# Storing the third pair's rows and gathering the first expert's tokens one step earlier

## The chip, the cores and the metric

The kernel runs on one core of a Trainium2 chip. The metric is the time of one execution on the device in microseconds (us), as the median of several runs. Beside it stands one execution under the hardware profiler; its span runs from the first to the last instruction.

## The reference

Two blocks follow each other. The first is attention with a sliding window of 128 and a linear position bias: 8 batches, 8 heads, 576 positions, head dimension 64.

```python
scores = scale * np.matmul(q, k.transpose(0, 1, 3, 2))
scores = np.where(mask, scores + bias[None], -1e9)   # 0 <= rel < 128
attn = softmax(scores)
x = np.matmul(attn, v)                                # to (4608, 512)
```

The second is a mixture of 8 experts that drops no token. Each of the 4608 tokens goes to the one expert with the largest logit.

```python
logits = x @ w_gate
expert_idx = np.argmax(logits, axis=1)
h = np.maximum(x_sorted[lo:hi] @ w1[e], 0.0)          # 512 -> 1024
y_sorted[lo:hi] = h @ w2[e]                           # 1024 -> 512
out = gate_w[:, None] * y                             # gate_w: softmax probability of the chosen expert
```

## The kernel before

**Attention.** The work is cut into 16 units: 4 pairs of batches, and for each pair 4 pairs of heads. A unit has 4 groups of key blocks, so there are 64 steps, i = 4 x unit + group. In a step, PE forms the scores of the step two ahead (`scores`, L756), ACT takes their exponential (L762), DVE multiplies by the bias factors (L765, for the last group of a unit L770), and PE multiplies the probabilities of this step by the values (`values`, L791). Twice in a unit, at groups 2 and 3, `finish` copies the result to `xT` on ACT (L808, L810) and adds up the probabilities on PE (L823), which DVE takes into `sumT` (L834).

The order of all instructions is written out by hand: a manual schedule. Each engine runs its own instructions in that order, so one that waits holds back all later ones on its engine. PSUM tiles called `m` come from a pool of two (`ps_m`), and the score tiles `sp` from another pool of two.

**Work behind the attention.** When a pair is done, `behind(bp)` returns a list of portions, which `some()` takes one at a time, one in each of the next steps. They hold the routing of the pair that is done: gate logits (`gate`, L843, L848), their turning to token rows (`turn`, L867), the choice of the expert (`scale_a` to `scale_c`), the place of each token in its expert's list (`count`, `place`), one-hot matrices (`ones_at`, L974 to L983) and the lists themselves (`enlist`, matmuls at L993, sum at L1000).

They also hold the storing of the pair's 9 row tiles, of 128 tokens each. `row_turned` transposes four blocks on PE (L1007) and copies them to the tile `xs` on ACT (L1009). `row_out` adds the scales on POOL (L1016) and stores the tile to the DRAM tensor `x_rows` by a DMA that POOL issues (L1021, two for the last tile). `row(bp, t)` does both. The `xs` tiles come from a pool of 4, so tile t reuses the buffer of tile t - 4 and waits for its store.

For the third pair (`bp == 2`, whose portions run in steps i = 48 and on) the list is another one, because the first expert's tokens are taken from the first three pairs alone. `early_table` (a matmul at L1069, small DVE instructions L1071 to L1073, then L1040 to L1047) makes the list `g_idx`, and `gather` issues four indirect DMAs on POOL (L1152), each of which fetches 128 rows of `x_rows` into `xg`. The gather waits for all stores of rows and for `g_idx`.

**Tokens of the first expert.** In the last unit, `prepare(fixed[0])` adds portions: for each of the four gathered blocks a scaling on DVE (`to_scale`, L1164, tile `xn`) and a turning (`to_columns`: four transposes on PE at L1177, a copy to `xgT` on ACT at L1178), then four sums on DVE (L537 to L540). The scaling of block j + 1 shares a portion with the turning of block j. What is left of the portions after step 63 is run by `while tasks: some()`.

**Experts.** Each expert's two layers are Strassen products of 7 multiplications (`strassen1`, L1357 and L1414, into the PSUM tiles `pair0a` to `pair2b`; `strassen2`, L1469). During the first expert the routing of the fourth pair is done (`with_tail`). The load of the first expert's w2 (L565 on SP) follows the end of the attention, whose memory it takes over.

Of the kernel before, what the change touches and what calls it, by code (L numbers as in the profile page):

```python
# [457 lines left out]
def kernel(  # L458
# [25 lines left out]
    TPB = 2 * S // P  # L484
# [18 lines left out]
    x_d = nc.dram_tensor("x_rows", (N, NA * PW), F32, kind="Internal").ap()  # L503
    x_pieces = x_d.rearrange("n (a w) -> (n a) w", a=NA)

    with ExitStack() as fast:
# [50 lines left out]
        def load_w1(g, w_pool, parts=None):  # L557
            if "w1" not in g:
                g["w1"] = w_pool.tile([P, DB, F], F32, name="w1")
            a = parts or slice(0, DB)  # L560
            nc.sync.dma_start(g["w1"][:, a], g["src"][0].rearrange("(a p) f -> p a f", p=P)[:, a])
# [5 lines left out]
        fixed = [dict(e=e, n=NJ, c0=e * NJ, src=(moe_w1[e], moe_w2[e]), pool=mx_pool) for e in range(E)]  # L567
# [23 lines left out]
        units = [(bp, hp) for bp in range(BP) for hp in range(HP)]  # L591
# [22 lines left out]
        def load_part(u, g):  # L614
            if g == 0:
                load_k(u, 0, S, nc.sync)
            elif g == 1:
                load_q(u, 0, S, nc.sync)
            else:
                load_v(u, g - 2, nc.gpsimd if u in (6, 7) else nc.sync)  # L620
# [14 lines left out]
        def no_earlier_than(there):  # L635
            nc.sync.dma_start(pace[:], there)
# [53 lines left out]
        def placed(bp, t):  # L690

            b = 2 * bp * S
            if t < 8:
                return [(0, P, b + t // 4 * S + t % 4 * P)]
            return [(0, KB, b + 4 * P), (KB, KB, b + S + 4 * P)]
# [44 lines left out]
        def table_consts():  # L740
            K["cols"] = iota("cols", [P, P], [[1, P]], 0, 0)
            K["thr"] = iota("thr", [P, NF], [[P, NF]], CAP, 0)
            K["xth"] = iota("xth", [P, XU], [[1, XU]], 1, 0)
            K["e_of"] = iota("e_of", [P, E, NF], [[1, E], [0, NF]], 0, 0)
# [92 lines left out]
        def gate(bp, c):  # L837
            if bp not in gs:
                gs[bp] = xp.tile([P, 2 * S], F32, name="gs", bufs=1)
            ps = ps_m.tile([P, 512], F32, name="m")  # L840
            c0, n = ((0, LQ), (LQ, LQ), (2 * LQ, P))[c]
            for hp in range(HP):
                nc.tensor.matmul(  # L843
                    ps[32 * hp : 32 * hp + 32, :n], lhsT=wgd[:, hp, :], rhs=xT[bp][:, hp, c0 : c0 + n],
                    start=True, stop=True,
                )
            if c < 2:
                nc.vector.tensor_tensor(gs[bp][:, c0 : c0 + n], ps[:, :n], sumT[bp][:, :LQ], op=ALU.add)  # L848
            else:
                nc.vector.tensor_tensor(  # L850
                    gs[bp][:, c0 : c0 + n].rearrange("p (b q) -> p b q", b=2),
                    ps[:, :n].rearrange("p (b q) -> p b q", b=2),
                    sumT[bp][:, None, LQ:].to_broadcast([P, 2, S - LQ]), op=ALU.add,
                )
# [5 lines left out]
        def turn(bp, part):  # L860

            if part == 0:
                gsr[bp] = small.tile([P, TPB, P], F32, name="gsr")
            t0, n = ((0, 4), (4, 4), (8, 1))[part]
            ps = ps_m.tile([P, 512], F32, name="m")
            for k in range(n):
                nc.tensor.transpose(ps[:, k * P : (k + 1) * P], gs[bp][:, (t0 + k) * P : (t0 + k + 1) * P], ident[:])  # L867
            nc.scalar.copy(gsr[bp][:, t0 : t0 + n, :].rearrange("p t c -> p (t c)"), ps[:, : n * P])
# [135 lines left out]
        def row_turned(bp, t):  # L1004
            ps = ps_m.tile([P, 512], F32, name="m")
            for hp in range(HP):
                nc.tensor.transpose(ps[:, hp * P : (hp + 1) * P], xT[bp][:, hp, t * P : (t + 1) * P], ident[:])  # L1007
            xs = xs_of[bp, t] = rows.tile([P, NA, PW], F32, name="xs")
            nc.scalar.copy(  # L1009
                xs[:, :, :PD].rearrange("p a (h f) -> p h a f", h=HP), ps.rearrange("p (h a f) -> p h a f", h=HP, a=NA),  # L1010
            )

        def row_out(bp, t):

            xs = xs_of.pop((bp, t))
            nc.gpsimd.tensor_copy(  # L1016
                xs[:, :, PD:].rearrange("p (r x) h -> p r x h", r=2),
                es_of[bp][:, t].unsqueeze(2).to_broadcast([P, 2, 2, HP]),
            )
            for p0, n, r0 in placed(bp, t):  # L1020
                nc.gpsimd.dma_start(x_d[r0 : r0 + n, :], xs[p0 : p0 + n].rearrange("p a w -> p (a w)"))  # L1021

        def row(bp, t):
            row_turned(bp, t)
            row_out(bp, t)
# [113 lines left out]
        def in_rows(g):  # L1139
            return g["n"] == NJ and g["e"] < NR  # L1140

        def gather(g, src):
            nm = "" if g["n"] == NJ else "1"
            g["xg"] = g["pool"].tile([P, g["n"], NA, PW], F32, name="xg" + nm)
            for j in range(g["n"]):
                c = g["c0"] + j
                if in_rows(g):
                    todo = [(g["xg"][:, j].rearrange("p a w -> p (a w)"), src, g_idx[:, c : c + 1])]
                else:
                    todo = [(g["xg"][:, j, k, :], x_pieces, p_idx[:, c - NR * NJ, k : k + 1]) for k in range(NA)]  # L1150
                for to, where, idx in todo:
                    nc.gpsimd.indirect_dma_start(  # L1152
                        out=to, out_offset=None, in_=where, in_offset=bass.IndirectOffsetOnAxis(ap=idx, axis=0),
                    )
# [66 lines left out]
        def behind(bp):  # L1221

            g3 = [lambda k=k: gate(bp, k) for k in range(3)]
            t3 = [lambda k=k: turn(bp, k) for k in range(3)]
            rs = [lambda t=t: row(bp, t) for t in range(TPB)]
            a, b, c, n, p, o, e = (
                [lambda f=f: f(bp)] for f in (scale_a, scale_b, scale_c, count, place, ones_at, enlist)
            )
            if bp == 2:
                return [g3, t3, a, b + [lambda: row_turned(bp, 0)], c + n + [lambda: row_turned(bp, 1)],  # L1230
                        [lambda: row_turned(bp, 2)], p + [lambda t=t: row_out(bp, t) for t in range(3)], o + rs[3:4],
                        rs[4:6], e + rs[6:7], [early_table] + rs[7:9], [lambda: gather(fixed[0], x_d[: 3 * 2 * S, :])]]
            turned = [lambda t=t: row_turned(bp, t) for t in range(2)]
            outs = [lambda t=t: row_out(bp, t) for t in range(2)]
            return [g3[0:1], g3[1:2], g3[2:] + t3[0:1], t3[1:], a, turned[0:1], b, turned[1:2], c + n + outs,
                    rs[2:3], p + rs[3:4], rs[4:5], o, rs[5:6], rs[6:7], e + rs[7:9]]
# [3 lines left out]
        def some():  # L1240
            if tasks:
                for f in tasks.pop(0):
                    f()
# [10 lines left out]
        for i in range(NG):  # L1254
            u, g = divmod(i, 4)
            bp, hp = units[u]
            no_earlier_than(prob[min(i + 1, NG - 1)][0:1, 0, 0:1])
            if u + 2 < len(units):
                load_part(u + 2, g)
            if u in (5, 6) and g % 2 == 1:  # L1260
                d = 2 * (u - 5) + g // 2
                load_w1(fixed[0], w1_a, slice(d, d + 1))
            if i == 1:
                token_numbers()
                table_consts()
            if g == 2:
                values(u, 0, (4,))
                finish(u, 0)
                some()
            if i + AHEAD < NG:  # L1270
                scores(i + AHEAD)
            if u in (10, 11):
                ws_tasks.pop(0)()
            if g == 0:
                values(u, 0, (0, 1))
                if u < HP - 1:
                    factors(u + 1)
            elif g == 1:
                values(u, 0, (2, 3))
            elif g == 2:  # L1280
                values(u, 1, (3, 4, 5))
            else:
                values(u, 1, (6, 7, 8))
                finish(u, 1)
            if u == len(units) - 1 and g == 1:
                tasks.extend(t for _, t in prepare(fixed[0]))
            if g != 2:
                some()
            if g == 3 and hp == HP - 1 and bp < BP - 1:
                tasks.extend(behind(bp))  # L1290
# [240 lines left out]
        for i in range(len(groups)):  # L1531
            g = groups[i]
# [67 lines left out]
```

## Time and profile before

| | before |
|---|---|
| median of 6 runs | 730.11 us (726.02 to 732.91) |
| the profiled execution, its own time | 726.64 us |
| its span | 724.8 us |
| granted TensorE clock, mean | 0.978 |
| PE busy | 676.6 us, 93% |
| DVE busy | 364.8 us, 50% |
| ACT busy | 206.2 us, 28% |
| POOL busy | 227.9 us, 31% |
| share of PE in the chain that ended last | 76% |
| stores of rows, L1021 on POOL | 40, 21.8 us |

All times of the trace count from the start of the span. "Busy" is the time in which an engine works on some instruction. An idle time is given with its releaser, the instruction whose end let the waiting one start; "issue" means that the profile shows nothing that was waited for. The matmul's ends are modelled, so lengths of single matmuls overlap. The DMAs that POOL issues are listed on POOL with the time that issuing takes, not with the time until they land.

### The profile page before, as it was taken

The numbers are of one execution on the slowest core, as the hardware profiler recorded it, in microseconds if no ns is written. First come the engines' busy times: TensorE is split into PE (matmuls) and PEld (weight loads), VectorE is DVE, ScalarE is ACT, GpSimd is POOL, SyncE is SP. The second block draws the span as 40 slices with busy tenths as digits, with TensorE's granted clock in tenths as the row PEclk, the third lists the DMA queues.
The fourth block names the chain that finished last, engine by engine and source line by source line (L and its number), as shares of the span: only waits on it lengthen the run. The fifth ranks groups of instructions, "written<-read, shape, count | busy, mean of one in ns | idle before, by whom it ended". The sixth has DMA issues, their size and how long they took to land.

```text
span 724.8 us, 14624 instructions
## 1 busy us (share of the span) xinstructions
PE 676.6 (93%) x6096; PEld 563.2 (78%) x6096; DVE 364.8 (50%) x691; ACT 206.2 (28%) x379; POOL 227.9 (31%) x344
## 2 busy tenths in 40 slices
PE   6998999997999979998999899989997999899996
PEld 5877878786788868977787687868785978687884
DVE  4547569774666817531843373347236522842500
ACT  5655565554341211121102200311121012102310
POOL 8011204133032570246025502742271237022020
PEclk9999999999999989999899999999998999999998
DMA  9786977764268623572357228533833382366010
GB/s 255 210 212 190 320 219 239 226 208 117 91 216 305 203 55 122 174 269 52 117 197 251 48 114 288 167 126 100 304 99 131 116 306 58 125 209 227 1 48 18
DMA packets 56909, 122.00 MB, mean 168 GB/s; under 512 B 5345, under 2 KB 22529, under 8 KB 56834
## 3 DMA queue, kind: packets, MB, share of 16 engines
q1 hardware_dynamic: 44562, 89.17, 37.8%
q0 software_dynamic: 11120, 30.92, 13.0%
q8 instruction: 50, 0.82, 0.5%
q10 hardware_dynamic: 1152, 0.88, 0.4%
q14 instruction: 25, 0.20, 0.1%
HBM read 101.79 MB, written 19.96 MB: 168 GB/s over the span
## 4 chain that ended last, share of the span: by engine, by line
PE 76%; issue 10%; DVE 5%; DMA 3%; another core or an unknown queue 2%; ACT 2%; POOL 1%; SPq 0%; POOLq 0%; DVEq 0%; ACTq 0%
PE sp L756 5%; PE pair2b L1414 4%; PE at L791 4%; PE pair2a L1414 4%; PE pair0b L1414 4%; PE pair2a L1357 4%; PE pair0a L1414 4%; PE pair0b L1357 4%; PE pair0a L1357 4%; PE pair1b L1357 4%; PE pair1a L1414 4%; PE pair1b L1414 4%; PE pair2b L1357 4%; PE pair1a L1357 4%; PE m L823 3%
## 5 line engine op out<-in xcount | busy, mean ns | idle before, releaser
L1152 POOL DMA_INDIRECT xg<-x_rows,p_idx x124 | 123.8, 998 | 37.8 <-issue 36.9
L1437 POOL DMA_INDIRECT out_dram<-zo,s_idx x39 | 44.6, 1144 | 287.4 <-DVE zo L1428 163.0
L765 DVE TENSOR_TENSOR pe<-pe,fac 128x768 f32<-128x768 f32 x48 | 45.7, 956 | 41.0 <-ACT pe L762 40.9
L756 PE MATMUL sp<-q_sb,k_sb 64*64 64x192 f32 (+2 forms) x1152 | 57.5, 320 | 8.4 <-DMA q_sb<-in_qT_dram 6.8
L762 ACT ACTIVATE pe<-sp 128x768 f32<-128x768 f32 x64 | 52.0, 812 | 40.4 <-PE sp L756 32.6
L791 PE MATMUL at<-pe,v_sb 64*64 64x192 f32 (+2 forms) x1408 | 59.0, 286 | 1.7 <-DVE pe L765 0.7
L756 PEld LDWEIGHTS sp<-q_sb,k_sb 64*64 64x64 f32 x1152 | 41.0, 136 | 17.2 <-issue 7.3
L791 PEld LDWEIGHTS at<-pe,v_sb 64*64 64x64 f32 x1408 | 46.8, 135 | 8.2 <-issue 3.0
L1368 ACT ACTIVATE h<-h 128x512 f32<-128x512 f32 x32 | 20.2, 632 | 90.1 <-DVE h L1367 83.5
L1016 POOL COPY xs<-es 128x16 f32<-128x16 f32 x36 | 11.5, 320 | 78.3 <-DVE es L930 74.6
L1021 POOL DMA_DIRECT2D x_rows<-xs x40 | 21.8, 547 | 41.7 <-issue 18.1
L823 PE MATMUL m<-pe,ind 128*32 128x192 f32 (+2 forms) x704 | 30.2, 291 | 1.0 <-issue 1.0
L1009 ACT COPY xs<-m 128x512 f32<-128x512 f32 x36 | 20.6, 586 | 24.6 <-PE m L1007 9.7
L1164 DVE TENSOR_TENSOR xn<-xg 128x512 f32<-128x512 f32 x39 | 25.9, 669 | 2.9 <-DMA xg<-x_rows,g_idx 2.9
L823 PEld LDWEIGHTS m<-pe,ind 128*32 128x32 f32 x704 | 23.8, 111 | 3.3 <-issue 1.2
L1414 PE MATMUL pair1b<-w,h 128*128 128x256 f32 x72 | 18.3, 382 | 5.8 <-issue 5.8
L1007 PE MATMUL m<-ident,xT 128*128 128x128 f32 x144 | 21.8, 282 | 1.8 <-DVE sumT L834 1.5
L1180 DVE STREAM_TRANSPOSE xgT<-xn 128x512 f32<-128x512 f32 x31 | 22.0, 711 | 1.1
L1469 PE MATMUL pair2a<-w,h 128*128 128x512 f32 x48 | 21.1, 592 | 0.0
L537 DVE TENSOR_TENSOR w2s<-w 128x512 f32<-128x512 f32 x16 | 11.0, 687 | 20.0 <-DMA w<-in_moe_w_dram 20.0
L1414 PEld LDWEIGHTS pair1b<-w,h 128*128 128x128 f32 x72 | 13.5, 189 | 9.1 <-issue 7.5
L808 ACT COPY xT<-at 128x640 f32<-128x640 f32 (+1 forms) x32 | 18.8, 587 | 4.4 <-PE at L791 4.4
(364 smaller groups left out, 1402.6 us busy)
## 6 DMA issues: line engine op xcount, KB each, us to landing
w<-in_moe_w_dram SPq DMA_DIRECT2D x29, 2048.0 KB
k_sb<-in_kT_dram SPq DMA_DIRECT2D x15, 576.0 KB
q_sb<-in_qT_dram SPq DMA_DIRECT2D x15, 576.0 KB
x_rows<-xs POOLq DMA_DIRECT2D x32, 264.0 KB
v_sb<-in_v_dram SPq DMA_DIRECT2D x26, 288.0 KB
w<-in_moe_w_dram SPq DMA_DIRECT2D x4, 512.0 KB
xg<-x_rows,p_idx POOLq DMA_INDIRECT x124
v_sb<-in_v_dram POOLq DMA_DIRECT2D x4, 288.0 KB
```

The lines of the kernel that those rows point to most:

```text
L756: nc.tensor.matmul(sp[c * KB : (c + 1) * KB, r, c0 : c0 + n], lhsT=k_sb[u][hs, c, kb * KB : (kb + 1) * KB], rhs=q_sb[u][hs, c, kb * KB : k ...
L762: nc.scalar.activation(pe[:], sp[:, :, :GC], AF.Exp, scale=SCALE)
L765: nc.vector.tensor_tensor(pe.rearrange("p r (k c) -> p r k c", k=2), pe.rearrange("p r (k c) -> p r k c", k=2), fac[:, h0 : h0 + 2, None, ...
L791: nc.tensor.matmul(acc[r * D : (r + 1) * D, c, lo - q0 : hi - q0], lhsT=v_sb[u][c * KB : (c + 1) * KB, kb, r * D : (r + 1) * D], rhs=pe[c ...
L823: nc.tensor.matmul(sm[32 * j : 32 * j + 32, lo - q0 : hi - q0], lhsT=none[:] if pe is None else ind[:, hp, :], rhs=fac[:, 0, :KB] if pe is ...
L1007: nc.tensor.transpose(ps[:, hp * P : (hp + 1) * P], xT[bp][:, hp, t * P : (t + 1) * P], ident[:])
L1152: nc.gpsimd.indirect_dma_start(out=to, out_offset=None, in_=where, in_offset=bass.IndirectOffsetOnAxis(ap=idx, axis=0),)
L1164: nc.vector.tensor_tensor(xn[:], x, s.unsqueeze(3).to_broadcast([P, NA, HP, TQ]), op=ALU.mult)
L1180: nc.vector.transpose(to.rearrange("p h (k j) -> p k h j", j=TQ), xn[:])
L1357: nc.tensor.matmul(ps[:, f * 256 : (f + 1) * 256], lhsT=left[m][:, d, fb * P : (fb + 1) * P], rhs=right[m][:, d, :], start=(m in (1, 2, 5) ...
L1414: nc.tensor.matmul(ps[:, :256], lhsT=left[m][:, f, c * P : (c + 1) * P], rhs=right[m][:, f, :], start=(m in (1, 2, 5) and f == 0), stop=Tr ...
L1437: ins = nc.gpsimd.indirect_dma_start(out=out[:, :], out_offset=bass.IndirectOffsetOnAxis(ap=s_idx[:, g["c0"] + j : g["c0"] + j + 1], axis= ...
```

## The change

For the third pair, the portions are put together anew. The rows are turned earlier: rows 2 and 3 in one portion, rows 0 to 3 stored in the portion of `place`, rows 4 and 5 with `ones_at`, rows 6 to 8 in the next portion, so that all nine stand ahead of `enlist`. The portion of `enlist` and the one of `early_table` no longer contain rows, and the gather moves from a portion of its own into that of `early_table`. The list is one portion shorter: 11 instead of 12.

The portions of `prepare(fixed[0])` are added at the first group of the last unit instead of the second, so that the scaling of block 0 is in step 60 instead of 61, and one portion less is left after step 63.

```diff
             if bp == 2:
-                return [g3, t3, a, b + [lambda: row_turned(bp, 0)], c + n + [lambda: row_turned(bp, 1)],
-                        [lambda: row_turned(bp, 2)], p + [lambda t=t: row_out(bp, t) for t in range(3)], o + rs[3:4],
-                        rs[4:6], e + rs[6:7], [early_table] + rs[7:9], [lambda: gather(fixed[0], x_d[: 3 * 2 * S, :])]]
+                rt, ro = ([lambda t=t, f=f: f(bp, t) for t in range(TPB)] for f in (row_turned, row_out))
+                return [g3, t3, a, b + rt[0:1], c + n + rt[1:2], rt[2:4], p + ro[0:4], o + rs[4:6], rs[6:9], e,
+                        [early_table, lambda: gather(fixed[0], x_d[: 3 * 2 * S, :])]]
...
-            if u == len(units) - 1 and g == 1:
+            if u == len(units) - 1 and g == 0:
                 tasks.extend(t for _, t in prepare(fixed[0]))
```

The instructions are the same in kind and number, and their order on POOL and SP is the same; on PE, ACT and DVE they move.

## Prediction

> **What bounds the kernel now.** I read the page first: PE is busy 93% of a span of 724.8 us and holds 76% of the chain that ended last, so only what stops PE counts. The diff touches units 12 to 15 of the attention (about 134 to 185 us), so next came the chain of waits there. An index i below is a group of scores: i = 4 x unit + group, and i = 60 to 63 is the last unit.
>
> ```profile
> 168.61 0.34 PE at L791 x8
> 168.96 0.90 PE m L823 x20
> 169.86 2.37 another core or an unknown queue
> 172.23 1.36 issue
> 173.58 0.63 PE m L1177 x4
> 174.21 2.27 PE at L791 x48
> 176.48 1.48 PE m L823 x16
> ...
> 180.42 0.60 ACT xgT L1178
> ```
>
> Columns: start, length, what. Nothing runs on PE from 169.86 to 173.58, 3.72 us. The instruction that ends this is the first turning of gathered tokens (L1177). It waits for a DVE scaling (L1164), which waits for the gather. The timelines of DVE and POOL say why:
>
> ```profile
> 168.91 0.96 DVE L770 TENSOR_TENSOR pe<-pe,fac 128x768 f32<-128x768 f32 x1 [0.35 <-ACT pe L762]
> 172.75 0.69 DVE L1164 TENSOR_TENSOR xn<-xg 128x512 f32<-128x512 f32 x1 [2.88 <-DMA xg<-x_rows,g_idx]
> ```
>
> ```profile
> 154.21 0.54 POOL L1021 DMA_DIRECT2D x_rows<-xs  x1 [3.54 <-ACT xs L1009]
> ...
> 164.20 1.09 POOL L1021 DMA_DIRECT2D x_rows<-xs  x2 [0.29 <-POOL xs L1016]
> 168.70 1.04 POOL L1152 DMA_INDIRECT xg<-x_rows,g_idx  x1 [3.41 <-DVE pe L765]
> 170.05 0.97 POOL L1152 DMA_INDIRECT xg<-x_rows,g_idx  x1 [0.30 <-issue]
> ```
>
> The second of the last two stores is issued at about 164.75; the gather, which waits for the stores, starts at 168.70, 3.95 us later, and its first block is readable at 172.75, 4.05 us after that. The list it reads (g_idx, L1044) was ready at 162.09. So stores, not the list, hold the gather. The table by stage (PE, PEld, DVE, ACT, POOL, granted clock, DMA share, GB/s) shows a second cost:
>
> ```profile
> 172.00:174.00 2.00, 0.42 (x4) 0.42 (x4) 1.25 (x3) 0.00 (x0) 1.22 (x2) 1.00 0.72 209
> 174.00:176.00 2.00, 2.00 (x42) 1.68 (x44) 0.44 (x1) 0.59 (x1) 0.00 (x0) 0.68 0.58 177
> 176.00:178.00 2.00, 2.00 (x41) 1.60 (x34) 0.01 (x1) 0.65 (x2) 0.00 (x0) 0.50 0.01 2
> 178.00:180.00 2.00, 1.48 (x10) 1.09 (x11) 1.61 (x3) 0.77 (x2) 0.00 (x0) 0.96 0.35 84
> ```
>
> After the idle time the granted clock is halved for some 3.4 us. The 48 value matmuls took 2.27 us where 24 took 0.66 at 163.12, so 0.95 too much; the sums after them 1.48 against 0.79 at 165.08, 0.69 too much. Together 1.64 us.
>
> **The change, part by part.** Instructions are the same in number; they move.
>
> Rows. All nine row turns (L1007, 0.43 us of PE each once running) now stand before the list matmuls of i = 57, where six stood. PE gets no more work. Two small PE stalls are added. Rows 4 and 5 now stand together after i = 55, and row 5's PSUM bank is read until then by the sum of L834 (before: 152.80 to 153.22, later by the 0.43 of row 3): about 0.4. Row 8 needs the bank of row 6 copied by ACT (behind one exponential of 0.81): about 0.25. Adding the moved rows, the list matmuls (L993, before 156.85) start at about 158.5 and end at 160.63. From there row 6 (0.46), rows 7 and 8 (1.07) are gone, and so is the wait of those rows for L1071 (160.65 to 161.23). The scores of i = 60 start at about 161.95 instead of 162.31: **0.36 gained**.
>
> Stores. There are four row buffers, so the copy of row 8 on ACT waits for the landing of row 4's store; behind that copy ACT holds the exponential of i = 59. Row 4's store is issued at about 154.0 (its copy is at the place of the old row 3, whose store is the 154.21 above). With 3.95 it lands at 157.95. Row 8 is copied by 158.55 (0.59), and its two stores are issued at 158.85 and 159.4 (0.55 each). The exponential ends at 159.4 and its factors on DVE at 160.4; PE reads them only in i = 59, past 163.6, so this stall is covered by some 3 us. POOL gets the same instructions in the same order; each row costs it 1.06 (0.21, 0.30, 0.55), and its wait for buffers has only further rows behind it. Last landing: 159.4 + 3.95 = 163.35.
>
> Gather. The list is ready 1.42 after the sums of i = 58 in the trace (160.67 to 162.09); these now end at 161.83, so 163.27. List and stores meet at 163.4, where the gather starts, 5.3 earlier. First block at 163.4 + 4.05 = 167.45; the others 1.27 us apart (the POOL rows), the last at 171.3.
>
> All this rests on how long a store takes to land. The trace gives two more cases: with loads around them, in pairs 0 and 1, the buffer of row 0 came back 5.08 and 6.67 us after its store's start (68.29 to 73.37, 112.69 to 119.36 in the POOL timeline). I take 3.95, because the loads of this pair end at about 155 (the last v_sb issue is at 152.29) and the rows that count are stored after it; 6.67 is kept for the range.
>
> The Trainium skill (DMA: Bandwidth & Descriptors, Anatomy of one DMA) gives a transfer from POOL about 2.0 us plus bytes over 436 GB/s, an estimate of 2.3 us for these halves of 132 KB. The trace has 3.95 here. By the page the stores would land at 161.7 and the list alone would set 163.4; the sum would not move.
>
> Tokens. The scaling of block 0 stands on DVE between the factors of i = 62 and 63, and its turning on PE before the values of i = 62. Factors of i = 62: before 167.60 to 168.57, now 0.36 earlier, so to 168.21. The scaling (0.69) then runs 168.25 to 168.92 with 0.8 us to spare on the gather. PE is ready at 167.95 (before it waited 0.31 here) and stands until 168.97: about 1.0 of idle. Then, from rows at full clock: turning 0.43, values 0.28, sums 0.92, turning 0.43, values 1.31, sums 0.80, turning 0.43, ending at 173.57. The last scaling waits on DVE behind L834 of the last sums (173.14 + 0.44), runs 0.69, and the last turning is over at 174.8. ACT's last copy (L1178) starts at 174.85 instead of 180.42: **5.57 gained** in all, 0.36 of it from the rows, some 1.64 from the clock.
>
> What follows hangs on that copy: the four sums of L537 to L540 (181.04 to 183.66), gate, pair0b at 184.74, then a chain nearly all PE. The load of w2 (L565, 178.03) was released by the last attention sums (177.96) and moves to about 173.2; its first reader is at 196.22, so it stays covered. I know no later event that stays where it is.
>
> I take off 0.4 for the gather's margin, since POOL starts have twice come right after a long DVE instruction ended (168.70 after 168.57; a copy of L1016 took 0.96 at 154.74 beside L983). **5.2 us**: the span becomes 719.6 and this execution 721.4 instead of 726.64. The median of the runs, 730.11, is 3.5 above the profiled one; I take the gain from it unchanged: **724.9 us**.
>
> The page TensorE: Matmul & The Clock Gate of the Trainium skill (Part 1) says the clock drops after an idle window of about 3.4 us that runs free of the kernel. A gap of 3.72 holds a whole such window in 9% of phases (an estimate), so most executions would lose nothing to the clock and the gain would be 3.7. The trace speaks against so strict a rule: PE worked from 173.58, and the clock fell past 174 all the same.
>
> **The rivals.** About 0.5%, 3.65 us, is what a measurement of this kernel can tell from no change.
>
> A, as above. Against it: it needs the gather by 168.25.
>
> B, row buffers hold the last stores back. If row 4's store takes 6.67, it lands at 160.7, row 8's stores go out until 162.15, land at 166.1, and the first block comes at 170.15, 1.9 late. PE loses 1.9; should the longer idle time again cost the clock, 1.64 more. Gain 3.7 to 2.0 less the margin: 726.8 to 728.1. For it: pair 1's row. Against it: no loads remain.
>
> C, slower. The scaling now stands ahead of the factors of i = 63 on DVE, and the turning ahead of the last values on PE, so a late gather stops everything, with less attention work left than before to hide it. Every us past 168.25 costs one. With 1.64 of clock the gain is gone when the block comes at 172.2. If both landings take 6.67 (160.7, then 162.15 + 6.67 = 168.8), it comes at 172.85, and the sums of i = 58 wait 0.4 for row 8's bank: 5.57 - 4.6 - 1.64 - 0.4 is a loss of 1.1, 731.2. From about 175.8 it is over 0.5%, some 734.
>
> D, the change moves this stage and the end doesn't follow. The chain has later holes on PE (3.61 at 263.93, 7.71 at 337.20, 7.05 at 542.72); should their ends not move with PE, they take the gain: 730.1. Against it: POOL's gathers run through them, issued after PE's own steps.
>
> **How the numbers follow.** A has 0.66, B 0.20 (0.03 of it still faster), C 0.10 (0.04 within the bound), D 0.04. So faster 0.69, same 0.25, slower 0.06. A alone, with a landing one us earlier or later and the six runs spread over 726.02 to 732.91 (a median of six is good to about 1 us), gives 723 to 727. The range takes in B and part of D: 722.3 to 729.3.
>
> **What would show it.** Right: the first gather at about 163.4, first L1164 near 168.3, no hole over 1.2 us on PE between 165 and 175, clock 1.00 there, last L1178 near 174.85, pair0b near 179.2. Wrong: an L1009 copy with over 2 us idle before it around 156 to 161, the first gather past 166, L1164 again waiting for the DMA, or the gain there at 185 and gone by 345.

## The result

The changed kernel's median is 728.18 us (34 runs, 723.27 to 735.65), that of the kernel before in the same comparison 729.23 us (71 runs, 721.53 to 742.01). The ratio is 0.9989 with a 95% interval of 0.9972 to 1.0007: no difference that can be measured. The profiled execution has a span of 725.1 us (before 724.8) and a mean granted clock of 0.981 (before 0.978). I had forecast 5.2 us less. That 728.18 lies inside the range that I gave (722.3 to 729.3) is luck: its upper end was only 0.8 us below the 730.11 of the kernel before. Ratios, here and below, take the executions that are at most 1.5% above the fastest of their kernel; medians take all.

The trace of after comes 1.73 us later into the changed part than that of before (the reciprocal of L888: 140.88 against 139.15); times below are therefore taken from the first row store of the third pair (L1021 on POOL: 147.77 before, 149.50 after), which has the same 1.73 between the two. The chain of waits of after, over the stretch where the forecast had a running PE:

```profile
164.36 0.32 PE m L1069 x2
...
167.45 0.47 PE m L823 x8
167.93 0.29 issue
168.22 0.54 PE m L823 x6
168.76 0.28 issue
169.04 0.43 PE m L823 x4
169.48 0.29 issue
...
178.03 0.63 PE m L1177 x4
...
182.83 0.59 ACT xgT L1178
```

The hole of 3.72 us in front of L1177 is gone, and no DMA stands in the chain any more: the tokens are there in time. But in the middle of one group of sums (L823), which waits for nothing, PE now does 4 to 8 matmuls and then nothing for about 0.3 us ("issue"), again and again. What POOL and the waiting engines did:

```profile
166.18 1.04 POOL L1152 DMA_INDIRECT xg<-x_rows,g_idx  x1 [3.50 <-DVE tb L1046]
...
170.47 0.95 POOL L1152 DMA_INDIRECT xg<-x_rows,g_idx  x1 [0.30 <-issue]
```

```profile
171.24 0.48 ACT L808 COPY xT<-at 128x384 f32<-128x384 f32 x1 [2.89 <-PE m L823]
```

The same copy in before, with no wait:

```profile
165.20 0.48 ACT L808 COPY xT<-at 128x384 f32<-128x384 f32 x1
```

The gather starts 16.68 us after the first store instead of 20.93, and the gaps begin 1.75 us after it. ACT's copy of the values (L808) starts at 171.24, although the last value matmul ended at 167.45 by the profile, which models the ends of matmuls: what waits for PE is released late too. The first sign comes 0.4 us ahead of the first gap: the exponential of i = 61 starts 1.99 us after that of i = 60 (167.54), in before 1.31. The table by stage (PE, PEld, DVE, ACT, POOL, granted clock, DMA share, GB/s):

```profile
164.00:166.00 2.00, 2.00 (x60) 1.78 (x54) 1.42 (x9) 0.67 (x2) 0.00 (x0) 1.00 0.04 13
168.00:170.00 2.00, 1.20 (x15) 0.52 (x15) 0.96 (x1) 0.36 (x1) 1.69 (x2) 1.00 0.74 192
170.00:172.00 2.00, 1.29 (x17) 0.65 (x14) 0.00 (x0) 0.65 (x2) 1.12 (x2) 1.00 0.66 203
172.00:174.00 2.00, 2.00 (x27) 2.00 (x31) 0.65 (x2) 0.81 (x1) 0.00 (x0) 0.50 0.47 135
```

PE gets through 15 and 17 matmuls in 2 us instead of 60, at a clock of 1.00, and then the clock halves. In the kernel before, the gather began at 168.70 and PE had already stopped at 169.86 to wait for it: a slow stretch like this one would have lain inside the wait, where it costs nothing.

Three sections of the way show where the gain went. The exponentials of i = 60 and i = 63 (L762 on ACT) are the marks between; all from the timelines, in us:

| | first store to i = 60 | i = 60 to i = 63 | i = 63 to last L1178 | sum |
|---|---|---|---|---|
| before | 15.41 | 4.88 | 12.36 | 32.65 |
| forecast | 15.05 | 4.88 | 7.15 | 27.08 |
| after | 16.05 | 9.94 | 7.34 | 33.33 |

The last section brought what was forecast. The middle one, for which the forecast had no change, took 5.06 us back.

### The profile page after: what moved, and what is told of

It is laid out like the page before. It is cut to its first block, busy times and chain, and to the rows that moved or that the text cites. A ratio compares the mean times of both kernels' runs of the same rounds, so it can differ in the third digit from the quotient of the medians.

```text
span 725.1 us, 14622 instructions
## 1 busy us (share of the span) xinstructions
PE 677.7 (93%) x6096; PEld 562.4 (78%) x6096; DVE 364.9 (50%) x691; ACT 206.5 (28%) x379; POOL 230.3 (32%) x344
## 4 chain that ended last, share of the span: by engine, by line
PE 74%; issue 11%; DVE 5%; DMA 4%; another core or an unknown queue 2%; ACT 2%; POOL 1%; SPq 0%; POOLq 0%; DVEq 0%; ACTq 0%
PE sp L756 5%; PE pair0a L1414 4%; PE pair2a L1414 4%; PE pair1a L1414 4%; PE pair2b L1414 4%; PE pair0b L1414 4%; PE pair2b L1357 4%; PE pair0b L1357 4%; PE at L791 4%; PE pair0a L1357 4%; PE pair1b L1414 4%; PE pair2a L1357 4%; PE pair1b L1357 4%; PE pair1a L1357 4%; DMA q_sb<-in_qT_dram 3%
## 5 line engine op out<-in xcount | busy, mean ns | idle before, releaser
L756 PE MATMUL sp<-q_sb,k_sb 64*64 64x192 f32 (+2 forms) x1152 | 59.7, 325 | 11.3 <-DMA q_sb<-in_qT_dram 7.9
L765 DVE TENSOR_TENSOR pe<-pe,fac 128x768 f32<-128x768 f32 x48 | 45.8, 958 | 44.1 <-ACT pe L762 43.9
L762 ACT ACTIVATE pe<-sp 128x768 f32<-128x768 f32 x64 | 52.0, 812 | 46.1 <-PE sp L756 40.7
L756 PEld LDWEIGHTS sp<-q_sb,k_sb 64*64 64x64 f32 x1152 | 42.7, 139 | 20.5 <-issue 8.2
L1021 POOL DMA_DIRECT2D x_rows<-xs x40 | 21.9, 548 | 36.0 <-issue 14.6
L823 PE MATMUL m<-pe,ind 128*32 128x192 f32 (+2 forms) x704 | 30.4, 287 | 0.9 <-issue 0.9
L823 PEld LDWEIGHTS m<-pe,ind 128*32 128x32 f32 x704 | 23.2, 110 | 4.0 <-issue 2.0
L1164 DVE TENSOR_TENSOR xn<-xg 128x512 f32<-128x512 f32 x39 | 26.0, 669 | 0.0
L1414 PE MATMUL pair1b<-w,h 128*128 128x256 f32 x72 | 19.1, 387 | 4.1 <-issue 4.0
L1180 DVE STREAM_TRANSPOSE xgT<-xn 128x512 f32<-128x512 f32 x31 | 22.0, 711 | 1.1
L1414 PE MATMUL pair0a<-w,h 128*128 128x256 f32 x64 | 17.3, 413 | 4.6 <-ACT h L1386 3.3
L808 ACT COPY xT<-at 128x640 f32<-128x640 f32 (+1 forms) x32 | 18.8, 587 | 8.6 <-PE at L791 5.7
```

The costliest lines, as they stand in the source:

```text
L756: nc.tensor.matmul(sp[c * KB : (c + 1) * KB, r, c0 : c0 + n], lhsT=k_sb[u][hs, c, kb * KB : (kb + 1) * KB], rhs=q_sb[u][hs, c, kb * KB : k ...
L762: nc.scalar.activation(pe[:], sp[:, :, :GC], AF.Exp, scale=SCALE)
L765: nc.vector.tensor_tensor(pe.rearrange("p r (k c) -> p r k c", k=2), pe.rearrange("p r (k c) -> p r k c", k=2), fac[:, h0 : h0 + 2, None, ...
L823: nc.tensor.matmul(sm[32 * j : 32 * j + 32, lo - q0 : hi - q0], lhsT=none[:] if pe is None else ind[:, hp, :], rhs=fac[:, 0, :KB] if pe is ...
L1164: nc.vector.tensor_tensor(xn[:], x, s.unsqueeze(3).to_broadcast([P, NA, HP, TQ]), op=ALU.mult)
L1180: nc.vector.transpose(to.rearrange("p h (k j) -> p k h j", j=TQ), xn[:])
```

## The experiments

Three theories stood for the gaps: (1) POOL's work on indirect gathers holds PE up, (2) PE runs dry because a code block is being fetched at that place (a code packet of 16 KB starts at 167.23 in after, and one at 169.73 in before, where PE stopped), (3) the DMA traffic itself. Ratios are to runs of the kernel before on the same chip, with 95% intervals. "Sections" are the three of the table above and their sum.

**Four plain loads from SP.** In `gather`:

```diff
+                if g is fixed[0]:
+                    nc.sync.dma_start(todo[0][0], src[j * P : (j + 1) * P, :])
+                    continue
```

> The changed kernel, with the first expert's four indirect gathers replaced by four plain loads of the first 512 rows of x_rows, issued from SP (this leaves out the choice of the first expert's tokens). Same bytes, same place in the program, no list read; they start when the stores have landed, about 164.3 instead of 166.18. In the changed kernel PE ran in bursts of 4 to 8 matmuls with 0.28 us between them from 167.93 to about 172.3, and the clock fell to 0.50 after. Theory 1 (POOL's work on the indirect gathers holds PE up): no such gaps, clock 1.00 to 180, first scaling near 169, last L1178 at about 177 instead of 182.83, and the time 4 to 6 us under the changed kernel: 722 to 724. Theory 2 (a code block is fetched at that place of PE's program, 167.23, and PE runs dry): the gaps stay within 1 us of where they were, last L1178 at 181 to 183, time 726 to 729. Theory 3 (the traffic of the transfers themselves): the gaps stay, about 2 us earlier, time 726 to 729.

Sections 16.04, 4.88, 7.73, sum 28.65; ratio 0.9954 (0.9915 to 0.9993). Not one gap, at a higher DMA share than the gather ever reached:

```profile
166.00:168.00 2.00, 2.00 (x64) 1.91 (x60) 1.74 (x9) 0.98 (x2) 0.00 (x0) 1.00 1.00 342
168.00:170.00 2.00, 2.00 (x64) 1.79 (x60) 1.61 (x3) 1.18 (x3) 0.00 (x0) 1.00 0.23 84
```

PE does 64 matmuls in 2 us with all DMA engines busy: theory 3 falls for plain transfers. A packet of code starts at 168.15, 17.67 us after the first store as in after (17.73), without effect. Against the kernel before the medians are 2.4 us apart and the ratio says 3.4; the expectation, 4 to 6 under the changed kernel, which differs from before by nothing measurable, was too high.

**Four plain loads from POOL.** As above with `nc.gpsimd.dma_start`, behind a POOL copy that reads `g_idx`.

> The changed kernel, with the same four plain loads of the first 512 rows of x_rows issued from POOL instead of SP, after a small POOL copy that reads the list g_idx, so that they start as the gathers did, at about 166.3 (the choice of the first expert's tokens is left out). It tells an indirect DMA from any DMA issued by POOL. Theory 1a (the indirect form alone holds PE up): no gaps on PE, as with SP, last L1178 at 177 to 178, time 722 to 725. Theory 1b (any DMA that POOL issues): the gaps stay while POOL issues the four, last L1178 at 179 to 183, time 725 to 729; against 1b stand POOL's row stores at 149 to 163, beside which PE had no such gaps. Theory 2 (code block): gaps stay at the same place. Theory 3 (traffic): gaps stay.

Sections 16.07, 4.88, 7.74, sum 28.69; ratio 0.9980 (0.9933 to 1.0027), by itself unclear. The loads start at 170.74, 16.55 after the first store, just when the gather did, and PE keeps its pace beside them:

```profile
170.74 2.19 POOL L1155 DMA_DIRECT2D xg<-x_rows  x4
```

```profile
172.00:174.00 2.00, 2.00 (x64) 1.78 (x59) 1.35 (x3) 1.09 (x4) 0.93 (x2) 1.00 0.92 287
```

So not every DMA of POOL's does it; the indirect ones do.

**Code moved by a whole block, then by half.** 64, then 32 small matmuls ahead of `scores(0)`:

```diff
+        for _ in range(64):      # second kernel: 32
+            nc.tensor.matmul(ps_blank[:32, 0:1], lhsT=blank[:], rhs=blank[:, 0:1], start=True, stop=True)
```

> The changed kernel with 64 matmuls of one column (and their weight loads, 128 PE instructions in all) added at PE's very start, where it waits 4.02 us for q and k. Code reaches PE in packets of 16 KB about every 256 recorded instructions (161.47, 167.23, 177.46 in the changed kernel's DMA rows, before 169.73); so all later packets move by half their distance: about 164.5 and 171 to 172. Theory 1 (POOL's gathers): the gaps stay where the gather is, from about 1.7 us after its start, last L1178 at 181 to 183 but for the start's offset, time within 1 us of the changed kernel. Theory 2 (code): the gaps move with the packet, to begin about 171 or to vanish, with last L1178 at 176 to 180 and the time 2 to 5 us lower. Theory 3 as theory 1.

> As the code shift before, but with 32 added matmuls, since 64 had put 256 PE instructions (each became two matmuls and two weight loads) in front, a whole code block, and the packet came at the same place again (176.50, gaps from 176.76). Now 128 instructions, half a block: the packet near the gather moves by about 3 us against the steps. Theory 1 (POOL's gathers): gaps on PE from about 1.75 us after the gather's start, for about 4.5 us, wherever the packet lies; the way from the first row store to the last L1178 stays at 33.0 to 33.4 us (33.33 in the changed kernel, 33.06 with the whole shift). Theory 2 (code fetched while the gather is generated): the gaps begin within 0.7 us of a packet's start, so about 3 us earlier or later, or are gone; that way falls to about 29 to 32. The total is some 3 us above the changed kernel by the added matmuls, whatever the theory.

The first missed its aim: 64 matmuls became 256 instructions, one whole block, and the packet fell on the same place (176.50). Sections 16.03, 9.67, 7.36, sum 33.06; ratio 1.0046 (1.0004 to 1.0089), with the added matmuls. The second moved the packet to 170.57 and the next to 179.44; the gather started at 171.87, and the chain shows:

```profile
173.21 0.43 PE m L823 x4
173.64 0.32 issue
173.95 0.55 PE m L823 x6
174.50 0.29 issue
```

The gaps begin 1.77 us after the gather again, and 3.07 after the packet. Sections 16.05, 8.45, 7.74, sum 32.24; ratio 1.0030 (0.9996 to 1.0063). The next packet comes when the gaps are over, and the kernel with plain loads has a packet at this place without gaps: theory 2 falls. In this execution the clock did not fall behind the gaps:

```profile
176.00:178.00 2.00, 1.45 (x14) 0.61 (x16) 0.00 (x0) 0.65 (x2) 0.95 (x1) 1.00 0.64 175
178.00:180.00 2.00, 2.00 (x62) 2.00 (x60) 1.13 (x2) 1.05 (x2) 0.00 (x0) 1.00 0.44 137
```

The middle section is 8.45 instead of 9.94, so the gaps, with the late releases in them, cost 3.57 and the halved clock some 1.5 where it comes.

**Rows and gather early, turning left where it was.** The condition of `prepare(fixed[0])` back to `g == 1`.

> Half of the change: rows, lists and gather early as in the changed kernel, but the turning of the tokens left where it was, in the steps from i = 61. Theory 1: the gather still takes PE's time from about 167.9 to 172, now in the middle of attention work that used to run undisturbed, and the first turning comes later, so this half alone loses against the kernel before by 0 to 2 us: last L1178 at 181 to 184, time 728 to 731. Theory 2 the same, if the packet falls at the same place. If nothing held PE up, as my prediction had it, the tokens would be there in time, no hole on PE, and the time would be 3 to 5 us under the kernel before.

Sections 16.06, 8.44, 7.95, sum 32.45. Ratio 0.9934 (0.9891 to 0.9977), while the medians (741.03 and 739.81) stand the other way round: as a time inconclusive, and its profiled execution is among its longest (744.32). The gaps are there with the tokens turned later, so the new place of the turning isn't their cause.

**Two gathers instead of four.** Blocks 2 and 3 as plain loads from SP.

> The changed kernel with two of the first expert's four gathers (blocks 2 and 3) replaced by plain loads of rows 256 to 511 from SP (this leaves out the choice of those tokens). POOL issues two indirect gathers instead of four. Theory 1: the gaps last about 2.5 us less (each gather takes 1.27 to 1.66 us of issue on POOL); from the first row store to the last L1178 30.5 to 31.5 us, half way between 33.33 and the 28.65 of four plain loads; the time 1 to 3 us under the changed kernel. If the mere presence of one gather costs all (a fixed cost), 33; if the first two cost nothing, 28.7.

Sections 17.33, 6.35, 7.75, sum 31.43; ratio 0.9977 (0.9948 to 1.0007). The middle section is the test: 1.47 us lost with two gathers, 3.57 with four, 0 with none. About 0.7 to 0.9 us for each. The first section is 1.3 longer than in the other runs for another reason, a row store that came back late:

```profile
153.52 7.96 DMA x_rows<-xs
...
170.65 0.52 PE m L823 x5
171.18 0.35 issue
```

ACT's copies of rows wait for buffers there, which is the mechanism of rival B. The gaps begin 1.77 us after the gather (169.41) here too.

**A quarter of the bytes.** Each gather reads 132 values from `x_pieces`, plain loads from SP bring the rest.

```diff
+                    to, where, idx = todo[0]
+                    nc.sync.dma_start(to[:, PW:], src[j * P : (j + 1) * P, PW:])
+                    todo = [(to[:, :PW], x_pieces[: 3 * 2 * S, :], idx)]
```

> The changed kernel with each of the four gathers reading a quarter of a row (132 of 528 values, from x_pieces by the same list, so that other data than the tokens come) and the other three quarters brought by plain loads from SP. Same count of indirect instructions and of list entries, a quarter of their bytes. Theory 1 (the generation of 128 entries for each gather on POOL, not the bytes): gaps as in the changed kernel, 33 to 33.5 us from the first row store to the last L1178. Theory 3' (the scattered reading of the rows themselves): gaps a quarter as long, 29 to 30.5 us.

Sections 16.04, 10.60, 7.34, sum 33.98; ratio 0.9998 (0.9959 to 1.0037). PE falls to 18 matmuls in 2 us here too, at a DMA share of 0.32 where after had 0.66 to 0.74:

```profile
170.00:172.00 2.00, 1.25 (x18) 0.55 (x14) 0.34 (x1) 0.81 (x1) 1.66 (x2) 1.00 0.32 69
```

The clock halves behind the gaps as in after. A quarter of the gathered bytes costs no less. Together with the kernel of two gathers: it is the number of gathers of 128 entries, not the bytes.

**Four more gathers in steady attention.** At i = 46, rows of v by a list 0 to 127, into tiles that nobody reads.

> The changed kernel with four more indirect gathers of 128 rows of v (512 values each, by a list 0 to 127 made at the start) into four tiles that nobody reads, put at i = 46, before the third pair's rows: POOL is free there from about 136. Nothing waits for them. Theory 1: PE in steady attention work (53 to 65 matmuls in 2 us at clock 1.00 there) falls to 15 to 20 in 2 us for about 4.5 us, beginning 1.5 to 2 us after the first of them starts; the steps behind come 2 to 4 us later and the time is 2 to 4 us above the changed kernel. Theory 2 (code): gaps only if a packet falls there. Theory 3 (traffic): the loads already hold the DMA engines at a share of 0.85 to 0.95 there without any gaps, so less than 1 us. If the slow-down needs DVE or POOL to be idle or PE's waiting on this very list, none.

```profile
131.63 1.33 POOL L1244 DMA_INDIRECT vx<-in_v_dram,seq  x1 [0.31 <-issue]
```

```profile
130.00:132.00 2.00, 2.00 (x48) 1.66 (x42) 1.97 (x4) 1.34 (x3) 0.91 (x2) 1.00 1.15 227
134.00:136.00 2.00, 1.58 (x13) 0.63 (x12) 1.38 (x2) 0.00 (x0) 1.39 (x3) 1.00 0.98 329
136.00:138.00 2.00, 0.51 (x8) 0.42 (x9) 0.00 (x0) 0.00 (x0) 1.70 (x4) 0.85 0.92 335
140.00:142.00 2.00, 2.00 (x11) 2.00 (x11) 0.77 (x2) 0.00 (x0) 0.00 (x0) 0.50 1.07 220
```

Nothing waits for these gathers, and PE falls from 48 matmuls in 2 us to 13 and 8. The first gap in the chain is at 133.81, 2.2 us after the first gather. Ratio 1.0160 (1.0091 to 1.0230), 11.8 us above the kernel before: far over the 2 to 4 expected. From the exponential of i = 48 to that of i = 51 it took 18.98 us where after took 10.76, so 8.2 us are lost right there. Behind the gaps the clock stayed at 0.50 from 138 to 146 and POOL's row stores of the pair before came late (145.96, behind 7.79 us idle); what each of these is worth isn't shown. The list is 0 to 127 in order, so the gaps don't need scattered rows.

**The turning alone.** The kernel before with `g == 0` in the condition of `prepare(fixed[0])`.

> The other half of the change alone: the kernel before with only the turning of the tokens put at i = 60, rows, lists and gather where they were. Theory 1 (POOL's gathers hold PE up): the gather starts when it did (20.9 us after the first row store in the kernel before), with PE's small steps not yet done but waiting behind the first turning; the first scaling waits for the gather, PE stands about 3 to 5 us, but most of the gather then lies in that idle time, so the way from the first row store to the last L1178 is 32 to 35 us against 32.65 before and 33.33 after; time 0 to 3 us above the kernel before. By my prediction's sum without theory 1 (tokens 25 us after the first store, three us later than PE could use them): 31 to 32.

Sections 15.41, 4.88, 13.06, sum 33.35; ratio 0.9993 (0.9951 to 1.0034). The chain waits for the gather, as theory 1 expected:

```profile
175.32 3.50 DMA xg<-x_rows,g_idx
```

The middle section is untouched since the gather starts after it. The prediction's sum without theory 1, 31 to 32, is missed.

**Fewer gathers in the expert stage.** If POOL's gathers hold PE up, the six later bursts of 20 (25 us each) should as well. In both kernels they go with waits like this one of after, where DVE waits 7.71 us for a completion of pair2b while PE first goes on with L1357 and L1414 and then stops and starts (3.1 us idle between 341.5 and 346.5). It comes late in the burst: POOL's first gather started at 316.86, and PE keeps 10 or 11 of these longer matmuls in 2 us until 340.

```profile
334.88 1.28 PE pair2b L1357 x3
336.15 0.02 issue
336.18 0.69 DVE h L1367
336.87 7.71 another core or an unknown queue
344.58 0.02 issue
```

The first kernel gathers all eight experts by rows. The second also splits each burst in two groups of four. The third is the kernel before with both edits.

```diff
-    NR = 2
+    NR = 8
...
-                fill.append((g, [next_groups, lambda: pieces(slice(NJ, E * NJ), "1")]))
+                fill.append((g, [next_groups]))
...
-            for a in ahead:                          # second and third kernel
+            for a in ahead[:1]:
                 gather(a, x_d[:, :])
             (strassen1 if big else plain1)(g)
+            for a in ahead[1:]:
+                tick = wk_pool.tile([P, 1], F32, name="tick")
+                nc.gpsimd.tensor_copy(tick[:], g["h"][:, 4, 256:257])
+                gather(a, x_d[:, :])
```

> The changed kernel with all eight experts' tokens gathered by whole rows (NR = 8; four gathers each and PE turns them, as for experts 0 and 1) instead of 16 gathers of quarter rows, so that each later burst has 8 indirect gathers (10 us of POOL) instead of 20 (25 us). PE gets 16 turnings more in each of six experts, 4 x 0.63 = 2.5 us each, 15 us in all. Theory 1: PE's holes at the bursts (before: 3.61 us at 263.93 and 7.71 at 337.20 after 18 to 21 us of a burst, with the halved clock behind them, about 7 us for each of six bursts) go or shrink to under 2 us: time 15 to 30 us under the kernel before. Rival: the holes belong to places in the program or to waits of its own, not to POOL's issue: they stay, and the time is 10 to 20 us above.

> As the kernel with all rows, and in each burst the four gathers of the next whole expert start only when a POOL copy has read the h that the fifth product of L1357 (m = 7) writes, so two groups of 4 gathers some 15 us apart instead of 8 in a row. Theory 1, with an effect that builds up over a burst (PE ran undisturbed for the first 8 us of a burst of 20, and through the 4 gathers of expert 1): no holes at the bursts, 0 to 6 us under the kernel with all rows. If it is the number of gathers alone that counts: the same time as there.

> The kernel before with the same two edits as the paced kernel (all rows, two groups of 4 gathers), so that the changed order of rows and turning is compared again with later stages that do not hide anything: theory 1 gives the same time as the paced kernel within 1.5 us, since the gather's gaps eat the earlier start.

All rows: 709.65 us, ratio 0.9628 (0.9587 to 0.9669), some 27 us less. Split: 706.95 us, ratio 0.9616 (0.9588 to 0.9645). Both beat the two kernels by far; between them the split makes no clear difference. The first part of the page and the groups of one product, after and then split kernel (busy, mean ns; idle before, releaser):

```profile
PE 677.7 (93%) x6096; PEld 562.4 (78%) x6096; DVE 364.9 (50%) x691; ACT 206.5 (28%) x379; POOL 230.3 (32%) x344
```

```profile
L1414 PE MATMUL pair1b<-w,h 128*128 128x256 f32 x72 | 19.1, 387 | 4.1 <-issue 4.0
```

```profile
PE 672.8 (96%) x6184; PEld 564.0 (80%) x6184; DVE 349.2 (50%) x666; ACT 221.9 (32%) x403; POOL 158.9 (23%) x278
```

```profile
L1177 PE MATMUL m<-ident,xn 128*128 128x128 f32 x128 | 19.4, 274 | 1.3 <-DVE xn L1164 1.3
L1414 PE MATMUL pair1b<-w,h 128*128 128x256 f32 x72 | 17.0, 379 | 0.0
```

PE has 14.4 us of turnings more (19.4 against 5.0) and is still busy for less time, since the products are faster (the groups of L1414 with `w` and `h` have a mean of 379 to 380 ns, in after 380 to 452; mean clock 0.995 against 0.981); its idle time falls from 47.4 to 30.2 us. The attention still shows the gaps (sections 16.05, 8.43, 7.74 and 16.05, 8.50, 7.74). So the waits go when a burst has 8 gathers instead of 20. That the gathers' number alone does it isn't shown: the same edits move most of the turning from DVE (L1180, 22.0 us in after) to PE and ACT and leave out the list of quarter rows for these experts (`pieces`).

With the order of before and both edits: 709.50 us, ratio 0.9669 (0.9624 to 0.9713), sections 15.41, 4.88, 13.23. Against the split kernel's 0.9616 the intervals just overlap, so even here the change isn't clearly worth anything; 2.55 us between the medians is more than the 1.5 I allowed.

## Why the prediction was wrong, point by point

**Tokens: the step that failed.** "Then, from rows at full clock" took the matmuls of i = 60 to 62 at the rate that they had in the trace of before, where no gather ran beside them. With the gather moved under them, i = 60 to 63 took 9.94 us instead of 4.88: 3.57 for the gaps and late releases by the runs whose clock held (8.43 to 8.50 in four kernels), about 1.5 for the clock, whose 1.64 the forecast had counted as gained. With plain loads in the gather's place the section is 4.88 to the hundredth.

The trace of before held a sign of this. The hole that I quoted has a release by "another core or an unknown queue" at 172.23, on the semaphore that counts PE's completions: that of the sums (L823) which had ended at 169.86 came 2.37 us late, while POOL gathered. It cost nothing there, since the tokens for the first scaling (L1164) came only at 172.75, as I read it; but I passed over the late signal.

**Rows.** Forecast 0.36 gained, measured 0.64 lost, the same in all runs with this order but one. The two stalls are 0.27 (row 5's bank, forecast 0.4) and 0.37 (row 8's, forecast 0.25), as foreseen in place and sum. The gain set against them was too large: the wait for L1071 that I removed holds the two matmuls of L1069 (0.32, moved and not removed), and a row turned by itself after a stop takes 0.60 to 0.66 us where I took 0.43.

**Stores and gather.** The gather came 16.68 after the first store, forecast 15.63. POOL's last wait for a store ended at 165.3, the list at 165.83 (L1044), and the gather began at 166.18: the list decided, as the sums ended later. In before, the last wait for a store ended at 167.8 and the gather began 0.9 later, so of the 3.95 that I took for a store's landing some 3.0 were that; what held POOL for the rest isn't shown (the profile names DVE's L765). The stores' second half was issued at 162.14, and rival B's late landing did not come in this execution, though it did in that with two gathers.

**The turning.** From i = 63 to the last copy 7.34 (after) to 7.73 (plain loads), forecast 7.15, before 12.36: right in mechanism, a little small in size. At a clock of 1.00 four turnings take 0.63 and the 48 values 1.48, where I had 0.43 and 1.31. With 0.84 for the sums, the halved clock of before had cost 1.43, not 1.64.

**Sum.** Forecast -0.36 + 0 - 5.21; measured +0.64 + 5.06 - 5.02 = +0.68 in the profiled pair, and +0.64 + 3.57 - 4.62 = -0.41 by the run whose clock held. With both kinds among the executions, a ratio of 0.9989 fits this. The gain that is there without the gather's effect, 4.00 us of the way, shows in the ratio of 0.9954.

**The rivals.** The result falls among those for no change, but by none of the mechanisms that I named. C had a late gather that stops everything; the gather was earlier than before, and hurt while it ran. D had a gain that later holes take back; but this stage itself gained nothing that they could have taken. Of its three "holes on PE" only that at 263.93 is one; at 337.20 and 542.72 DVE waits and PE works on for 3.7 and 2.7 us. What I said against D, that POOL's gathers run through these places, is likely their cause, as the runs with fewer gathers suggest. Two sums were off by little: B's lower end is 728.5 with the margin, not 728.1, and without the clock's 1.64 a gain of 3.5 would be left, not 3.7.

## What to carry to other kernels

That POOL issues an indirect gather doesn't make it free for PE: beside this kernel's small matmuls, each gather of 128 entries cost 0.7 to 0.9 us of PE in one place, and four of them over 8 us in another, with a halved clock behind. Put gathers where PE waits anyway or does few, long matmuls, try few wide ones in place of many narrow ones, and read a hole whose releaser is unknown against POOL's timeline before calling it a wait for data. When a wait is removed, ask what had been lying inside it.

## What the runs showed of the hardware

Beside POOL's indirect gathers, from 1.7 to 2.2 us after the first of them, PE does 8 to 18 matmuls in 2 us where 48 to 64 went before, in the midst of groups that wait for nothing, and ACT and DVE are released late by it (they wait 2.89 us, in the expert stage 7.71). The loss follows the number of gathers and not their bytes, came in both places of the attention where PE worked beside them, and did not happen beside plain loads from SP or POOL at DMA shares up to 1.00. The four gathers for expert 1 (224.13 to 229.03 in after), beside matmuls of 0.22 us (1.73 for 8), left no hole in the traces of before, after and the kernels with all rows:

```profile
226.00:228.00 2.00, 2.00 (x14) 1.82 (x12) 1.80 (x13) 0.35 (x1) 1.48 (x2) 1.00 0.98 311
```

That is PE's full pace there, and no more than the 15 to 17 that got through beside the gather in the attention, so it doesn't show that these gathers leave PE alone. Bursts of 20 left holes near their end, and splitting a burst of 8 changed nothing that could be measured.

The Trainium skill (SBUF — State Buffer, Who interferes with whom) says that DMA never contends with a compute engine. The plain loads agree (64 matmuls in 2 us at a share of 1.00), the indirect ones don't (15 at 0.74). Which part of their issue holds PE up, the entries that POOL makes or the way they reach the DMA engines, stays open. So does whether the recording of the trace has a part in it: every execution here was one whose spans and clock were recorded.

The clock fell to 0.50 behind stretches in which PE was busy for 1.20 to 1.29 of 2 us, not idle, in some executions (after, 172 to 174) and not in others with the same gaps (the half shift, 176 to 180; all rows, with PE busy for 1.21 of 174 to 176). What decides between the two isn't shown.
